# Spare products in TensorE's gaps, grouped transfers of the totals and a re-planned order, in a gated linear attention with a low-rank mixer behind it

## The chip, the cores and the metric

The kernel runs on one core of one Trainium2 chip. The metric is device time in microseconds (us), the median of several executions; lower is better. The engines are TensorE (PE, with its weight loads shown as PEld), VectorE (DVE), ScalarE (ACT), GpSimd (POOL) and SyncE (SP), which here only issues transfers. All data is float32. L12 is line 12 of the kernel whose profile is read.

## The reference

Two stages follow each other. The first is an attention with a complex gate, for 4 batches, 8 heads, 768 steps, 48 channels:

```python
mag = np.sqrt(a_re * a_re + a_im * a_im)
scale = np.minimum(mag, 0.999) / (mag + 1e-06)
a_re_n, a_im_n = (a_re * scale, a_im * scale)
for t in range(S):
    new_re = ar * S_re - ai * S_im            # ar, ai: step t of a_re_n, a_im_n
    new_im = ar * S_im + ai * S_re
    S_re, S_im = (new_re + k[t] outer v[t], new_im)
    y[:, :, t] = q[t] @ S_re
```

The second takes y as x (4 x 768 x 384) and mixes it, over time by a product of rank 32, and over channels by two layers (384 to 1536 and back):

```python
h = xt @ U @ V                                # xt: x with time last
u = x + h.transpose(0, 2, 1)
ch = np.maximum(u @ w_ch1, 0.0) @ w_ch2
return u + ch
```

## The kernel before

**Chunks.** Time is cut into chunks of 128 steps, 6 per batch, 24 in all. They are numbered 0 to 23. The gates are computed for groups of chunks: two groups of one chunk, then groups of two (`GROUPS`).

**Stages of the attention, per group or chunk.**
- `gates(g)`: magnitudes and logarithms of the gates on ACT and DVE (tiles x, y, l in GL, n); `within`: product `es ps` (L513) and two exponentials es; `totals`: products `tot` (L529), an exponential into E, and four transfers T<-E per chunk on SP's queue (L536), which put E's four blocks of rows into T's layout; `turns`: the angles z, then product `ph` (L569, and L572 for the carry of the first batch's chunks), then ACT and DVE make F, the fraction of a turn. From the second batch on a small transfer of POOL's queue adds the last row of F to the next chunk's z (z<-F, L563). `waves`: sine and cosine cs.
- `prep(i)`: DVE multiplies q and k by es and cs (qkc); PE transposes (`tr`, L618); ACT copies into QK.
- `chain(i)`: DVE multiplies QK by T at growing distances (L297); between them PE makes the products of the diagonal (`inner`, L652), `corners` (L699) and `corner` (L714), which go to AT, in part by way of DG and four transfers AT<-DG (L689); `ks ps`, `yT` (L748, L752), `dk` (L762) and G carry the state; `yr` (L777) turns the result back to xo.

**The mixing.** `mixer(m)` treats two chunks. Its first one of a batch needs all six chunks' xo (`rank`, L802). Then `mixed` (L814) and `uTp` (L821) make uT; 36 products `up` (L833, six at a time) with a Relu on ACT into h, and 12 `down` (L844) per chunk; DVE adds; POOL's queue writes the output (L850). The weights w1 and w2 are given as float64: `single` loads each panel as words (raw), six DVE operations turn them into float32, and a transfer of POOL's queue adds the remainder.

**What sets the order.** No loop above issues instructions. Each operation is given to `Plan` with its engine, a cost, what it reads and writes, the tiles it takes and a rank, and `Plan.order` simulates the five engines: whenever an engine is free, it picks among the operations that are ready and whose buffers are free the one with the lowest urgency (of the table `URGENCY`, by kind and number), and among those within 4 of it (`stay`) one of the same `way`, which is 1 for products that use a part of the array. The order found is issued as it is: every engine works through its own list, and an instruction waits there for its inputs with all that is behind it. The costs are formulas (`c_act`, `c_dve`, `c_dma`); `SP` adds 2.0 until a transfer lands, and `PE` multiplies by 1.3 for the first six chunks. "small" (the mixing's small steps) has urgency n - 1000, "mixing" (up, down) n + 1000, so that up and down are what PE does when it has nothing else. A buffer is taken in the plan by the first operation that reads or writes it.

Of the kernel before, what the change touches and what calls it, by code (L numbers as in the profile page):

```python
# [25 lines left out]
    "w1": {0: 22.6, 1: 16.9, 2: 21.7, 3: 31.9, 4: 26.8, 5: 7.2, 6: 29.2},  # L26
    "w2": {0: 30.9, 2: 32.1, 4: 29.2, 6: 36.2, 8: 31.1, 10: 46},
    "gates": {0: -14.2, 1: 4.3, 2: -3.3, 4: 4.1, 6: 26.6, 8: 13.4, 10: 16.1, 12: 17.5, 14: 17.8, 16: 24.3, 18: 23.5,
        20: 24.3, 22: 26.5},
    "angles": {0: -6, 1: 1.4, 2: 1.1, 4: -0.7, 6: 9.1, 8: 15.2, 10: 15.7, 12: 17.1, 14: 17.4, 16: 30.3, 18: 23.2,  # L30
        20: 12.9, 22: 26.4},
    "totals": {0: -98.9, 1: -100.2, 2: -95.1, 3: -104.8, 4: -93, 5: -92, 6: -97.8, 7: -99.3, 8: -88.1, 9: -93.3,
        10: -90.1, 11: -91, 12: -87.6, 13: -93.2, 14: -86.5, 15: -82.1, 16: -87.3, 17: -82.3, 18: -76.1, 19: -78,
        20: -75.7, 21: -76.5, 22: -77.2, 23: -78.7},
    "prep": {0: -3.4, 1: -6.1, 2: -1.7, 3: -0.5, 4: 1, 5: 2.1, 6: 8.3, 7: 9.2, 8: 10.3, 9: 11, 10: 13.2, 11: 14.9,
        12: 16.1, 13: 15.9, 14: 16.6, 15: 18.2, 16: 18, 17: 19.5, 18: 11, 19: 21, 20: 21.6, 21: 21.9, 22: 16.5,
        23: 33.7},
    "levels": {0: 0.6, 1: -3.8, 2: 0.6, 3: -1.7, 4: -1.9, 5: -1.5, 6: 8.4, 7: 8.6, 8: 6.8, 9: 14.9, 10: 12.7, 11: 13,
        12: 13.2, 13: 17.8, 14: 12.3, 15: 13.3, 16: 20.7, 17: 20.5, 18: 19.3, 19: 16.6, 20: 21.5, 21: 20.9, 22: 20.7,
        23: 28.2},  # L40
    "rest": {0: 7.1, 1: 3.2, 2: 4.6, 3: 6.2, 4: 5.8, 5: 6.4, 6: 7.8, 7: 13.7, 8: 16.8, 9: 17.2, 10: 14.8, 11: 18.2,
        12: 21, 13: 22.1, 14: 22.6, 15: 26, 16: 25.3, 17: 26.7, 18: 23, 19: 26.1, 20: 26.1, 21: 29.8, 22: 27.9,
        23: 30.6},
# [3 lines left out]
class Plan:  # L47
# [5 lines left out]
    def __init__(self, lag, change, stay, urgency):  # L53
        self.lag, self.change, self.stay, self.urgency = lag, change, stay, urgency
        self.ops, self.log, self.tag, self.bufs = [], {}, {}, {}
# [5 lines left out]
    def add(self, engine, cost, rank, f, reads=(), writes=(), late=0.0, way=0):  # L61
# [3 lines left out]
        need, uses = set(), set()  # L65
# [11 lines left out]
    def order(self):  # L77
# [15 lines left out]
        events, out, now = [], [], 0.0  # L93
# [16 lines left out]
        while True:  # L110
            for e in free:
# [17 lines left out]
                if pick:  # L129
# [15 lines left out]
            while events and events[0][0] <= now:  # L145
                _, n, landed = heapq.heappop(events)
                if landed:
# [8 lines left out]
        assert len(out) == len(ops), "the plan is stuck"  # L156
# [4 lines left out]
def kernel(  # L161
# [65 lines left out]
    plan = Plan(0.06, 0.12, 4.0, urgency)  # L227
# [44 lines left out]
    def ACT(*a, **kw):  # L272
        plan.add("ACT", *a, **kw)

    def DVE(*a, **kw):
        plan.add("DVE", *a, **kw)
# [4 lines left out]
    def SP(*a, **kw):  # L281
        plan.add("SP", *a, late=2.0, **kw)
# [7 lines left out]
    def switch(rank, name):  # L290
        table(1.28, rank, lambda: nc.scalar.preload_act_table_set(name))  # L291
# [668 lines left out]
```

## Time and profile before

| | |
|---|---|
| median of 3 runs | 792.26 us (790.36 to 792.93) |
| the profiled execution's own time | 786.05 us |
| its span, first to last instruction | 784.3 us |
| mean granted clock of TensorE | 0.961 of full |
| PE busy | 711.5 us (91%) |
| DVE, ACT, POOL busy | 428.9, 398.8, 45.3 us |
| first `up` on PE | 164.37 us after the span's start |
| T<-E, transfers | 96, of 48 KB each |

The profile is of one execution. Its page gives busy time by engine, the span in 40 slices with the granted clock of TensorE in tenths, the chain of work that ended last followed back from the last instruction, and groups of instructions with the idle time before them and what ended it. Its trace can be asked for the timeline of an engine, the waits of an engine by what ended them, and the busy time of all engines in given stretches. An f32 product stands in the records as two passes, a transpose as one. In the first 30 us the clock's record reads 1.00.

### The profile page before, as it was taken

The numbers are of one execution on the slowest core, as the hardware profiler recorded it, in microseconds if no ns is written. First come the engines' busy times: TensorE is split into PE (matmuls) and PEld (weight loads), VectorE is DVE, ScalarE is ACT, GpSimd is POOL, SyncE is SP. The second block draws the span as 40 slices with busy tenths as digits, with TensorE's granted clock in tenths as the row PEclk, the third lists the DMA queues.
The fourth block names the chain that finished last, engine by engine and source line by source line (L and its number), as shares of the span: only waits on it lengthen the run. The fifth ranks groups of instructions, "written<-read, shape, count | busy, mean of one in ns | idle before, by whom it ended". The sixth has DMA issues, their size and how long they took to land.

```text
span 784.3 us, 21460 instructions
## 1 busy us (share of the span) xinstructions
PE 711.5 (91%) x9522; PEld 535.4 (68%) x9522; DVE 428.9 (55%) x585; ACT 398.8 (51%) x686; POOL 45.3 (6%) x83
## 2 busy tenths in 40 slices
PE   2657877788989999999999999999999999999996
PEld 0435656566678868867876787676886867677683
DVE  5797988867859686585867883552623010010100
ACT  6586867665767686949596765241321202011010
POOL 4000000111000000000000000000000000000000
PEclk9857989899989999999999999999999999999999
DMA  8867536747432333333314312110100000000000
GB/s 192 188 129 160 100 90 138 152 120 161 89 79 43 73 70 70 76 58 70 80 38 106 69 37 55 42 26 11 41 1 18 11 11 11 20 1 21 10 11 20
DMA packets 165500, 52.89 MB, mean 67 GB/s; under 512 B 154784, under 2 KB 160416, under 8 KB 165408
## 3 DMA queue, kind: packets, MB, share of 16 engines
q1 hardware_dynamic: 161520, 41.87, 24.6%
q0 software_dynamic: 3888, 9.66, 5.1%
q8 instruction: 75, 1.23, 0.7%
q14 instruction: 17, 0.14, 0.1%
HBM read 33.59 MB, written 4.72 MB: 49 GB/s over the span
## 4 chain that ended last, share of the span: by engine, by line
PE 78%; DVE 7%; ACT 5%; DMA 4%; issue 4%; SPq 1%; POOL 0%; POOLq 0%; DVEq 0%; ACTq 0%
PE up L833 23%; PE down L844 22%; PE tr L618 5%; PE inner L652 5%; PE dk L762 3%; DVE QK L297 3%; PE ph L569 2%; PE yT L748 2%; PE es ps L513 2%; PE yT L752 2%; PE corner L714 2%; PE corners L699 2%; PE mixed L814 2%; PE ks ps L734 1%; PE tot L529 1%
## 5 line engine op out<-in xcount | busy, mean ns | idle before, releaser
L844 PE MATMUL down<-w,h 128*128 128x384 f32 x576 | 199.2, 489 | 0.0
L833 PE MATMUL up<-uT,w 128*128 128x256 f32 x864 | 196.9, 384 | 0.0
L297 DVE TENSOR_TENSOR QK<-QK,T 96x1024 f32<-96x1024 f32 (+1 forms) x144 | 169.6, 1186 | 20.4 <-PE corner L714 10.2
L833 PEld LDWEIGHTS up<-uT,w 128*128 128x128 f32 x864 | 162.8, 191 | 24.9 <-issue 1.0
L844 PEld LDWEIGHTS down<-w,h 128*128 128x128 f32 x576 | 104.9, 190 | 60.4 <-issue 0.2
L294 ACT ACTIVATE h<-up 128x512 f32<-128x512 f32 x72 | 42.9, 596 | 160.5 <-PE up L833 160.3
L652 PEld LDWEIGHTS inner<-QK 96*32 96x32 f32 x4608 | 48.3, 113 | 36.2 <-issue 26.2
L652 PE MATMUL inner<-QK 96*32 96x16 f32 (+1 forms) x4608 | 55.6, 192 | 13.6 <-DVE QK L297 8.8
L618 PE MATMUL tr<-ident,qkc 128*96 128x128 f32 x384 | 57.4, 291 | 10.9 <-DVE qkc L297 10.1
L300 DVE TENSOR_TENSOR xo<-mixed,xo 128x384 f32<-128x384 f32 x24 | 13.2, 555 | 95.5 <-PE mixed L814 94.7
L297 DVE TENSOR_TENSOR qkc<-qk,cs 128x768 f32<-128x768 f32 x48 | 45.8, 953 | 32.7 <-PE tr L618 23.2
L618 PEld LDWEIGHTS tr<-ident,qkc 128*96 128x96 f32 x384 | 44.4, 134 | 26.3 <-DVE qkc L297 10.0
L300 DVE TENSOR_TENSOR xo<-down,xo 128x384 f32<-128x384 f32 x24 | 13.3, 556 | 89.4 <-PE down L844 89.4
L621 ACT COPY QK<-tr 96x512 f32<-96x512 f32 x96 | 52.4, 581 | 18.4 <-PE tr L618 18.1
L658 DVE COPY_PREDICATED DG<-mask,inner 128x128 f32<-128x128 int32 (+1 forms) x72 | 24.6, 343 | 32.1 <-PE inner L652 29.9
L748 PE MATMUL yT<-AT,VP 128*64 128x128 f32 x384 | 37.7, 280 | 4.8 <-DMA AT<-DG 2.3
L779 ACT COPY xo<-yr 128x384 f32<-128x384 f32 x24 | 11.5, 478 | 56.1 <-DMA out_dram<-xo 50.7
L513 PE MATMUL es ps<-GL,mid 128*128 128x384 f32 x48 | 23.5, 599 | 15.2 <-DVE GL L500 14.0
L850 POOL DMA_DIRECT2D out_dram<-xo x24 | 13.5, 562 | 394.0 <-DVE xo L300 386.8
L762 PEld LDWEIGHTS dk<-VP,ks 128*96 128x96 f32 x320 | 31.7, 173 | 3.3 <-issue 2.0
L291 ACT ACT_TABLE_LOAD x26 | 33.4, 1283 | 1.2 <-PEq L944 0.7
L762 PE MATMUL dk<-VP,ks 128*96 128x48 f32 x320 | 33.1, 256 | 0.0
(93 smaller groups left out, 842.9 us busy)
## 6 DMA issues: line engine op xcount, KB each, us to landing
ar<-in_a_re_dram SPq DMA_DIRECT2D x24, 192.0 KB, 3.4
ai<-in_a_im_dram SPq DMA_DIRECT2D x24, 192.0 KB, 3.4
raw<-in_moe_w_ch_dram SPq DMA_DIRECT2D x6, 768.0 KB, 5.3
qk<-in_q_dram SPq DMA_DIRECT2D x24, 192.0 KB, 2.9
qk<-in_k_dram SPq DMA_DIRECT2D x24, 192.0 KB, 3.5
VP<-in_v_dram SPq DMA_DIRECT2D x24, 192.0 KB, 3.2
w<-cx POOLq DMA_DIRECT2D x12, 384.0 KB, 5.8
T<-E SPq DMA_DIRECT2D x96, 48.0 KB, 2.0
```

Of the source, the lines that this page charges most:

```text
L291: table(1.28, rank, lambda: nc.scalar.preload_act_table_set(name))
L294: return nc.scalar.activation(out=o, in_=i, func=f, **kw)
L297: nc.vector.tensor_tensor(out=o, in0=a, in1=b, op=OP.mult)
L300: nc.vector.tensor_tensor(out=o, in0=a, in1=b, op=OP.add)
L513: PE(0.65, R1, lambda: nc.tensor.matmul(out=get(*ps), lhsT=mid, rhs=of(l, i), start=True, stop=True), [l, ("mid", 0)], [ps, ("sums", g, i)])
L618: nc.tensor.transpose(out=get(*ps)[0:D2, j], in_=get(*qkc)[:, hh * HH + j].rearrange("p u d -> p (u d)"), identity=ident)
L621: ACT(c_act(HH * CH) - 0.05, R1, lambda u=u, hh=hh, ps=ps: nc.scalar.copy(out=get(*QK)[:, u, hh * HH:(hh + 1) * HH], in_=get(*ps)[0:D2]), ...
L652: nc.tensor.matmul(out=get(*ps)[js, h], lhsT=k_of(h)[:, js], rhs=part(q_of(h)[:, js], "p"), start=True, stop=True, tile_position=(0, j * BLK))
L748: nc.tensor.matmul(out=a[u * DP:(u + 1) * DP, p], lhsT=vv[:, h], rhs=get(*ATi)[:, h], start=True, stop=(c == 0), tile_position=(0, u * DP))
L762: nc.tensor.matmul(out=get(*dk)[0:D2, h], lhsT=get(*ks)[:, h], rhs=get(*VPi)[:, h, 0:D], start=True, stop=True)
L833: nc.tensor.matmul(out=get(*ps)[:, e], lhsT=w1[:, f, (ff + e) * 128:(ff + e + 1) * 128], rhs=get(*uT)[:, f], start=(f == 0), stop=(f == KD ...
L844: nc.tensor.matmul(out=get(*ps), lhsT=get(*h)[:, ff, cc * CH:(cc + 1) * CH], rhs=w2[:, ff], start=(ff == 0), stop=(ff == KF - 1))
```

## The change

1. **Spare products.** From 3 us of the plan's time on and until the first up, whenever PE has nothing to do in the plan, a product of the identity with itself is put there (cost 0.3). It writes a tile of PSUM that nobody reads. The order has 188 of them.
2. **Totals by group.** E and T hold a group; T has 3 buffers of a group in place of 6 of a chunk, E one of a group in place of two of a chunk. The four transfers move both chunks at once: 52 transfers in place of 96. They have a fixed urgency, as have the transfers AT<-DG (`"place"`), which stood at the rank of "rest".
3. **The plan's rules.** PE costs are no longer multiplied by 1.3 and have 0.17 until they land; ACT and DVE give 0.09 of their cost to landing; SP issues cost at least 0.65 and land 1.4 or 2.0 later; a product that follows on PE may start when the one before it has been issued. `takes`: a product takes the buffer that its result will go to. The operations on one ACT table may change places between two table loads.
4. **Loads.** U is loaded by one transfer for six, each panel of w2 by one for two.
5. **New numbers** for all kinds in `URGENCY`.

The order that comes out, at three places. First TensorE at the start of the program (es ps, tot and ph belong to the gates of chunk 0, tr to its q and k). Before:

```order
L513 MATMUL es ps<-GL,mid 128x384
L529 MATMUL tot<-total,GL 64x64 x8
L569 MATMUL ph<-z,prefix 128x384
L618 MATMUL tr<-ident,qkc 96x128 x16
L513 MATMUL es ps<-GL,mid 128x384
L652 MATMUL inner<-QK 32x32 x32
```

and in the change:

```order
L924 MATMUL spare<-ident 128x128 x20
L522 MATMUL es ps<-GL,mid 128x384
L548 MATMUL tot<-total,GL 64x64 x8
L924 MATMUL spare<-ident 128x128 x13
L580 MATMUL ph<-z,prefix 128x384
L924 MATMUL spare<-ident 128x128 x19
L630 MATMUL tr<-ident,qkc 96x128 x8
L924 MATMUL spare<-ident 128x128 x5
```

The real products stand in the same order, with runs of spare ones between them.

Second, TensorE around the first up, with the last products of the first batch's attention ahead of it (yr) and the mixing's rank, mixed and uTp. Before:

```order
L777 MATMUL yr<-ident,yTs 128x128 x4
L569 MATMUL ph<-z,prefix 128x384
L802 MATMUL rank<-xo,UV 32x384 x6
L814 MATMUL mixed<-r,V 128x384 x2
L821 MATMUL uTp<-ident,xo 128x128 x6
L569 MATMUL ph<-z,prefix 128x384
L833 MATMUL up<-uT,w_64 128x256 x12
```

and in the change:

```order
L815 MATMUL rank<-xo,UV 32x384 x6
L548 MATMUL tot<-total,GL 64x64 x8
L924 MATMUL spare<-ident 128x128
L827 MATMUL mixed<-r,V 128x384 x2
L924 MATMUL spare<-ident 128x128
L834 MATMUL uTp<-ident,xo 128x128 x3
L924 MATMUL spare<-ident 128x128
L834 MATMUL uTp<-ident,xo 128x128 x3
L924 MATMUL spare<-ident 128x128 x3
L846 MATMUL up<-uT,w_64 128x256 x6
L580 MATMUL ph<-z,prefix 128x384
L846 MATMUL up<-uT,w_64 128x256 x12
```

The two ph products (of chunks 6 and 7, whose z may come from POOL's queue) stood ahead of the first up and now stand behind its first six and its next twelve. Ahead of the first up PE has otherwise the same products in both.

Third, SP's queue where the first group of two chunks has its totals. Before:

```order
L396 DMA ar<-in_a_re_dram 128x8x48 x2
L396 DMA ai<-in_a_im_dram 128x8x48
L536 DMA T<-E 48x256 x8
L396 DMA ai<-in_a_im_dram 128x8x48
L423 DMA raw<-in_moe_w_ch_dram 128x1536
L423 DMA raw<-in_moe_U_dram 128x64 x6
```

and in the change:

```order
L535 DMA T<-E 48x2x256 x2
L701 DMA AT_99<-DG_100 32x8x32 x4
L535 DMA T<-E 48x2x256 x2
L409 DMA qk<-in_k_dram 128x8x48
L411 DMA VP_89<-in_v_dram 128x8x48
L402 DMA ar<-in_a_re_dram 128x8x48 x2
L402 DMA ai<-in_a_im_dram 128x8x48 x2
L430 DMA raw<-in_moe_w_ch_dram 128x1536
L430 DMA raw<-in_moe_U_dram 128x6x64
```

Eight transfers of totals became four, all of the group's gate loads (ar, ai) now stand behind them, and U is one transfer.

The diff, cut:

```diff
 URGENCY = {
-    "w1": {0: 22.6, 1: 16.9, 2: 21.7, 3: 31.9, 4: 26.8, 5: 7.2, 6: 29.2},
+    "w1": {0: 100.39, 1: -28.13, 2: 97.08, 3: 85.64, 4: 58.8, 5: 15.35, 6: 28.72},
...
-    "totals": {0: -98.9, 1: -100.2, 2: -95.1, 3: -104.8, 4: -93, 5: -92, 6: -97.8, 7: -99.3, 8: -88.1, 9: -93.3,
...
-    def add(self, engine, cost, rank, f, reads=(), writes=(), late=0.0, way=0):
+    def add(self, engine, cost, rank, f, reads=(), writes=(), late=0.0, way=0, takes=()):
...
-        need, uses = set(), set()
+        need, uses = set(), {a[:2] for a in takes}
...
+                    mixing = mixing or ops[n][3][0] == "mixing"
+                elif e == "PE" and now >= self.idle[0] and free[e] <= now and events and not mixing:
+                    out.append(-1)
+                    free[e] = now + self.idle[1]
+                    ways[e] = 0
+                    heapq.heappush(events, (free[e], -1, 0))
...
-                    if (ops[m][0] != ops[n][0] or ops[n][2] > 0) == bool(landed):
+                    if (ops[m][0] != "PE" or ops[n][0] != "PE") == bool(landed):
...
-        if kind == "totals":
+        if kind in ("totals", "place"):
             return n - 100
...
-    plan = Plan(0.06, 0.12, 4.0, urgency)
+    plan = Plan(0.04, 0.12, 4.0, (3.0, 0.3), urgency)
...
-    def PE(cost, rank, *a, **kw):
-
-        plan.add("PE", cost * (1.3 if rank[0] not in ("small", "mixing") and rank[1] < NCH else 1.0), rank, *a, **kw)
...
+    def PE(*a, **kw):
+        plan.add("PE", *a, late=0.17, **kw)
+
+    def ACT(cost, *a, **kw):
+        plan.add("ACT", cost - 0.09, *a, late=0.09, **kw)
+
+    def DVE(cost, *a, **kw):
+        plan.add("DVE", cost - 0.09, *a, late=0.09, **kw)
...
-    def SP(*a, **kw):
-        plan.add("SP", *a, late=2.0, **kw)
+    def SP(cost, *a, **kw):
+        plan.add("SP", max(cost, 0.65), *a, late=2.0 if cost > 0.65 else 1.4, **kw)
...
-        ACT(cost, rank, f, reads=reads, writes=list(writes) + [TABLE])
+        ACT(cost, rank, f, reads=list(reads) + [TABLE], writes=writes)
...
+        def totals():
+            e, tt = ("E", g), ("T", g)
+            buffer(e, "E", 1, [128, GC, HH, NTOT])
+            buffer(tt, "T", 3, [D2, GC, H * NTOT])
+            for i in range(lo, hi):
+                of_blocks(i)
+            for u in range(2):
+                for w in range(2):
+                    SP(0.65, ("totals", lo), lambda u=u, w=w: nc.sync.dma_start(
+                        out=get(*tt)[u * D:(u + 1) * D, 0:hi - lo, w * HH * NTOT:(w + 1) * HH * NTOT],
+                        in_=get(*e)[w * 64:w * 64 + D, 0:hi - lo].rearrange("p c h b -> p c (h b)")), [e], [tt + ((u, w),)])
...
-            SP(0.15, RR, lambda js=js: nc.sync.dma_start(out=get(*ATi)[js, :, js], in_=get(*DGi)[js]), [DGi],
+            SP(0.65, ("place", i), lambda js=js: nc.sync.dma_start(out=get(*ATi)[js, :, js], in_=get(*DGi)[js]), [DGi],
...
+    spare = []
+
+    def idle():
+
+        if not spare:
+            spare.append(pools["psM"].tile([128, 128], FP, tag="psM", name="spare", padded_shape=[128, 512]))
+        nc.tensor.matmul(out=spare[0], lhsT=ident, rhs=ident, start=True, stop=True)
     for n in plan.order():
-        plan.ops[n][4]()
+        (plan.ops[n][4] if n >= 0 else idle)()
```

More of the change, by code (lines that the diff above doesn't have):

```diff
@@ L92, in order @@
         have = set()
-        events, out, now = [], [], 0.0
+        events, out, now, mixing = [], [], 0.0, False
         def fits(n):
@@ L155, in order @@
                             heapq.heappush(ready[ops[m][0]], (rank[m], m))
-        assert len(out) == len(ops), "the plan is stuck"
+        assert len(out) == len(ops) + out.count(-1), "the plan is stuck"
         return out
@@ L671, in f @@
                 mul(qk, qk, tp)
[L672 removed]
+            DVE(c_dve((u1 - u0) * H * CH // 2), rank, f, [("T", group_of(i))], [QK])
         def grow(rank, hf, u0=0, u1=2):
```

112 lines of the change are left out of this document (51 added, 61 removed).

## The prediction

> **What bounds the kernel now.** I read the page first: the busy shares, the slices, and the shares of the chain that ended last.
>
> ```profile
> span 784.3 us, 21460 instructions
> PE 711.5 (91%) x9522; PEld 535.4 (68%) x9522; DVE 428.9 (55%) x585; ACT 398.8 (51%) x686; POOL 45.3 (6%) x83
> PE   2657877788989999999999999999999999999996
> PEclk9857989899989999999999999999999999999999
> PE 78%; DVE 7%; ACT 5%; DMA 4%; issue 4%; SPq 1%; POOL 0%; POOLq 0%; DVEq 0%; ACTq 0%
> ```
>
> TensorE is the bound, but not everywhere: its slices are full from about the twelfth on, and before that they stand at 2 to 9 tenths, with a granted clock that falls to half. So I asked for the busy time in stretches cut at the first product of the mixing (164.4 us), and for the end. Columns: stretch and length, busy time and instructions of PE, its weight loads, DVE, ACT, POOL, then the clock, the DMA share and GB/s.
>
> ```profile
> 0.00:40.00 40.00, 17.49 (x282) 11.01 (x282) 26.25 (x49) 25.06 (x45) 10.17 (x33) 0.91 0.81 190
> 40.00:100.00 60.00, 40.01 (x840) 31.60 (x840) 52.51 (x72) 48.93 (x80) 3.41 (x4) 0.77 0.62 130
> 100.00:165.00 65.00, 48.98 (x928) 35.83 (x929) 52.49 (x72) 41.92 (x72) 3.40 (x4) 0.88 0.55 127
> 164.00:784.00 620.00, 606.04 (x7475) 457.53 (x7474) 297.63 (x394) 283.25 (x490) 28.32 (x42) 0.99 0.21 47
> 761.85 15.64 PE L844 MATMUL down<-w,h 128*128 128x384 f32 x48
> 777.53 0.56 DVE L300 TENSOR_TENSOR xo<-down,xo 128x384 f32<-128x384 f32 x1 [7.18 <-PE down L844]
> ```
>
> Once the mixing has begun, PE is busy for 606.0 us of the 613 until its last product ends at about 777.4. That work is the same in both kernels. So the span is the time of the first mixing product, plus about 613 us of PE work, plus a fixed tail of 7 us (777.5 to 784.3). What the change is worth is how much earlier that first product comes (**first up**, below), and what it does to the 7 us of idle PE behind it.
>
> Ahead of first up no engine is full: PE 106.5 of 165 us, DVE 131.3, ACT 115.9. The chain of waits in that stretch alternates between them:
>
> ```profile
> by line: DVE QK L297 11.8%; issue 8.3%; PE tr L618 5.7%; PE ph L569 5.6%; DMA z<-F 4.5%; DVE qkc L297 4.5%; PE es ps L513 3.7%; PE inner L652 3.5%; ACT y L294 3.4%; ACT L291 3.1%; PE ph L572 3.1%; ACT x L294 2.4%; ACT GL L294 2.1%; DMA VP<-
> ```
>
> **Part 1: the clock ahead of first up.** The timeline shows the same groups at half and at full clock:
>
> ```profile
> 48.25 1.91 PE L618 MATMUL tr<-ident,qkc 128*96 128x128 f32 x8 [0.50 <-DVE qkc L297]
> 54.36 2.92 PE L513 MATMUL es ps<-GL,mid 128*128 128x384 f32 x4 [4.20 <-DVE GL L500]
> 57.22 2.16 PE L529 MATMUL tot<-total,GL 128*64 128x64 f32 x32
> 170.40 1.45 PE L513 MATMUL es ps<-GL,mid 128*128 128x384 f32 x4
> 174.38 1.15 PE L529 MATMUL tot<-total,GL 128*64 128x64 f32 x32
> 435.67 1.08 PE L618 MATMUL tr<-ident,qkc 128*96 128x128 f32 x8
> 438.47 0.60 PE L618 MATMUL tr<-ident,qkc 128*96 128x128 f32 x4
> ```
>
> tr goes from 1.91 to 1.08 us, es ps from 2.92 to 1.45, tot from 2.16 to 1.15. On the chain before 165 us, tr, es ps and the two ph lines hold 5.7 + 3.7 + 5.6 + 3.1 = 18.1%, or 29.9 us; nearly all of their pieces ran cold, and at the warm ratio (0.5 to 0.57) about 13 us of that goes, and with tot (1 us) and the cold pieces of dk, corners and ks (an estimate of 1 us) **15 us**. That is the upper end: all of it counts only if nothing else takes over. What can take over is DVE, which works 52.5 of the 60 us from 40 to 100. The lower end is 0, if DVE is the true bound there and PE's pieces stand on the chain by turns only. I take the middle, **-7.5 us**: DVE is idle for about 30 us before the first product of the mixing, some 7 of them at the start, before data is there.
>
> Do the spare products hold the clock up? Three stretches of 5 us say how little it takes to lose it:
>
> ```profile
> 125.00:130.00 5.00, 3.46 (x159) 3.08 (x159) 3.00 (x5) 3.46 (x5) 0.00 (x0) 1.00 0.53 134
> 130.00:135.00 5.00, 3.89 (x135) 3.46 (x131) 4.22 (x5) 2.03 (x5) 0.00 (x0) 1.00 0.70 131
> 135.00:140.00 5.00, 5.00 (x95) 3.23 (x94) 3.36 (x6) 2.59 (x7) 0.00 (x0) 0.66 0.67 125
> ```
>
> Busy for 7.35 of 10 us, PE is throttled in the next 5, though no single idle stretch there was long (the chain's waits inside it are of 1.5 us). The planned spare products stand in just such gaps, so I expect most, not all, of the clock.
>
> [...]
>
> **What the spare products cost.** There are 188, all ahead of first up. Eight tr against four cost 1.08 - 0.60 = 0.48 us more, so one pass of 128 columns takes 0.12 us. An f32 product is two passes (the page has 864 records for the 432 products of up), so a spare takes 0.24 us warm and, at tr's ratio, 0.43 us cold: 45 us in all warm, 81 cold. The room: PE's 106.5 us carry a cold surcharge of about 24 us (half-clock shares of 46% and 24% from the clocks 0.77 and 0.88; the first 40 us taken as cold), so the real work is 82.7 us, and a first up at about 149 leaves 66 us of gaps. 45 fits, with 21 to spare. Each spare stands where the plan sees PE idle for at least an instant, so a real product that comes early waits for at most the run ahead of it. I cost them at **0**; the price without that cover is the third rival. They stop at first up, so they take nothing from the 613 us.
>
> **Part 2: SP's queue.** Four transfers per group in place of eight. Before:
>
> ```profile
> 58.80 6.83 SPq L536 DMA_DIRECT2D T<-E  x8
> 65.67 0.58 SPq L396 DMA_DIRECT2D ai<-in_a_im_dram  x1
> 65.00:70.00 5.00, 2.69 (x76) 1.79 (x74) 1.88 (x2) 1.59 (x3) 0.85 (x1) 1.00 0.72 145
> ```
>
> Eight issues hold SP for 6.8 us (0.85 each), the load of ai stands behind them, and from 65 to 70 us PE, DVE and ACT are all mostly idle. Four fewer are 3.4 us at most on that place. The four now start only when both chunks' totals stand, and move twice the bytes, so part of it goes back. **-2 us**, between -3.4 and 0. U as one transfer for six and w2 as one for two save issues too; SP had idle time there, 0.
>
> **Part 3: what stands in front of first up.** The place itself, before:
>
> ```profile
> 153.53 2.61 PE L802 MATMUL rank<-xo,UV 128*32 128x384 f32 x12
> 156.75 1.56 PE L814 MATMUL mixed<-r,V 128*128 128x384 f32 x4 [0.61 <-ACT r L805]
> 158.31 1.19 PE L821 MATMUL uTp<-ident,xo 128*128 128x128 f32 x6
> 158.90 1.20 DVE L823 COPY uT<-uTp 128x384 f32<-128x384 f32 x2
> 162.96 1.62 PE L569 MATMUL ph<-z,prefix 128*128 128x384 f32 x2 [3.45 <-DMA z<-F]
> 164.37 5.98 PE L833 MATMUL up<-uT,w 128*128 128x256 f32 x23
> 149.66 0.95 DVE L548 SCALAR_TENSOR_TENSOR z<-x,n 128x768 f32<-128x768 f32 x1
> 154.25 0.55 DVE L575 SCALAR_TENSOR_TENSOR F<-F,ph 128x384 f32<-128x384 f32 x1 [0.59 <-ACT F L294]
> 154.98 0.96 DVE L300 TENSOR_TENSOR x<-x,y 128x768 f32<-128x768 f32 x1 [0.18 <-ACT y L294]
> 155.98 0.56 DVE L490 TENSOR_SCALAR x<-x 128x768 f32<-128x768 f32 x1
> ```
>
> The mixing's input uT is complete at 160.1, but PE stands in a ph that waits for its z (a transfer that lands late), so up starts at 164.37 and not at 160.2: **-4.2 us**, since in the change both late ph products stand behind the first six ups. If z is late there as well, PE waits in the mixing instead and the gain is 0; it is nearer to the full gain, because z's transfer then has the time of six ups more. The two ph products are work moved behind first up: 1.62 us cold, by es ps's ratio 0.8 us warm, so **+1.6 us** for both.
>
> DVE has the same work ahead of the first add of the mixing but for one z, one F, one sum and one clamp of x, which now come later: 0.95 + 0.55 + 0.96 + 0.56 = 3.0 us. As DVE is full for only part of this stretch I count half, **-1.5 us** (0 to -3).
>
> **Part 4: behind first up.** PE's waits there, the largest:
>
> ```profile
> PE yT L748 <- DMA AT<-DG: 2.3, 1, 2.3
> PE tot L529 <- issue: 1.6, 1, 1.6
> ```
>
> All of them make about 7 us. A new order may lose these or bring others of the same size; I take **0**, with -7 and +7 as bounds. The plan's durations, the buffers it takes early, E as one buffer of a group (where ACT must now wait for four transfers to land before the next group's exponentials) and the freer table order act only through the order; behind first up DVE has 298 and ACT 283 us of work in 620, which hides it. Were that cover gone, PE would wait for tr or inner inputs, as it does before 165.
>
> **Sum.** -7.5 - 2 - 4.2 - 1.5 + 1.6 = -13.6 us: first up at about 149, span 770.7 us. The profiled execution took 786.05 us in all (1.75 outside its span), so it would be 772.5; the runs shown have a median of 792.26, 0.8% above it, and I take the same 13.6 us from that: **778.7 us**.
>
> **Rivals.**
> - *DVE is the bound* and the clock is not. The clock's 7.5 and SP's 2 us go; 4.2 + 1.5 - 1.6 = 4.1 us stay: **788 us**. For it: 52.5 of 60 us. Against it: DVE's 30 idle us, and that PE's lines hold more of the chain than any.
> - *The clock is full from the start* and the whole 15 us come off: 792.26 - 13.6 - 7.5 = **771 us**. Against it: the throttling at 135 us, without a long gap, and DVE.
> - *Slower: the spares stay cold and PE falls behind its plan.* PE's demand ahead of first up is (82.7 + 45) us at full clock and, cold, 1.77 times that. With a half-clock share f it is 127.7 x (1 + 0.77 f): it overtakes 164.4 us at f = 0.37, which is a mean granted clock of about 0.81 up to first up. At 0.75 (f = 0.5) it is 177, 12.5 us later than before, with the 1.6 of ph **806 us**. For it: the clock was 0.77 from 40 to 100 with PE busy for two thirds. [...]
>
> **How the numbers follow.** Forecast 0.47 (between 772 and 785 by the ends of its terms), DVE the bound 0.24, full clock 0.15, cold spares 0.14. The range 764 to 790 holds the forecast, most of the full clock's case and of the DVE case: about 8 in 10. What a measurement of this kernel can tell from no change is 0.3%, 2.4 us: 789.9 to 794.6 is the same. Faster: 0.46 + 0.15 + 0.17 = 0.78. Same: 0.07 of the DVE case, and 0.02 of the others, 0.09. Slower: 0.13.
>
> **What would show it.** Right: a clock above 0.95 up to first up, tr x8 near 1.1 us at 50 us, first up between 145 and 153, and some 613 us from there to PE's last product. The clock at one and first up near 160 is DVE's case; a clock below 0.81 with spares right in front of late products is the slow one; new PE waits over 7 us behind first up would break the term I set to nothing.

## The result and the profile after

| | before | after |
|---|---|---|
| median | 791.31 us (788.90 to 792.93, 4 runs) | 767.96 us (766.59 to 773.01, 4 runs) |
| ratio | | 0.9721, 95% interval 0.9676 to 0.9765 |
| profiled execution, its span | 786.05, 784.3 us | 773.01, 771.2 us |
| second profile, its span | 789.77, 788.0 us | 765.88, 764.1 us |
| first up, in the two profiles | 164.37, 164.22 us | 150.71, 148.61 us |

The change makes the kernel 23 us faster. The forecast was 778.7 us, with 764 to 790 as its range. Before was run again beside the experiments, 7 to 17 executions at a time, and its medians were then 787.7 to 788.6 us; against these the gain is some 20 us.

The page of the changed kernel, with the span, the busy time by engine, the slices of TensorE and of its granted clock, and the group of the spare products:

```profile
span 771.2 us, 22118 instructions
PE 740.9 (96%) x9898; PEld 572.5 (74%) x9898; DVE 424.2 (55%) x585; ACT 393.4 (51%) x686; POOL 44.9 (6%) x83
PE   8989998997999999999999999999999999999996
PEclk9999898999999999999999999999999999999999
L924 PE MATMUL spare<-ident 128*128 128x128 f32 x376 | 57.6, 302 | 1.7 <-POOL ident masks.py:199 1.4
```

The first eleven slices of PE stood at 2 to 9 tenths and read 7 to 9 now, and the clock's slices there read 8 and 9, where they read 5 to 9. Take the 57.6 us of spares from the 740.9 and the same real products take 683.3 us, where they took 711.5. I put these 28.2 us down to the clock, since the same groups run in about half the time (es ps and tr, below). The span fell by 13.1 us only, so PE's gaps (idle and spares together) grew by 15.1, from 72.8 to 87.9 us. More than half of what the warmer TensorE saves is spent waiting for the others.

The stretches of the changed kernel (columns as in the prediction: PE, its weight loads, DVE, ACT, POOL, clock, DMA share, GB/s) and pieces of its timeline:

```profile
40.00:100.00 60.00, 54.22 (x1081) 45.07 (x1080) 52.19 (x72) 44.63 (x76) 2.57 (x3) 0.94 0.69 147
0.00:150.70 150.70, 135.67 (x2420) 116.00 (x2420) 124.49 (x186) 107.17 (x189) 16.27 (x40) 0.95 0.66 144
150.00:771.00 621.00, 605.90 (x7485) 457.07 (x7483) 300.29 (x402) 286.86 (x499) 28.61 (x43) 0.99 0.23 51
1.45 7.13 PE L924 MATMUL spare<-ident 128*128 128x128 f32 x40 [1.45 <-POOL ident masks.py:199]
9.79 0.88 PE L522 MATMUL es ps<-GL,mid 128*128 128x384 f32 x2 [1.21 <-DVE GL L509]
11.22 3.17 PE L924 MATMUL spare<-ident 128*128 128x128 f32 x26
36.40 1.04 PE L630 MATMUL tr<-ident,qkc 128*96 128x128 f32 x8
150.71 2.86 PE L846 MATMUL up<-uT,w 128*128 128x256 f32 x12
160.80 0.91 PE L580 MATMUL ph<-z,prefix 128*128 128x384 f32 x2 [1.41 <-DMA z<-F]
```

The clock from 40 to 100 us went from 0.77 to 0.94, tr from 1.91 to 1.04 us, the first es ps from 1.62 to 0.88 us, and first up waits for no z. One of the two ph waits now inside the mixing, 1.41 us. Behind first up this pair shows no gain: PE's last product ends 6.8 us ahead of the span's end in all four profiles, which gives 613.1 us before (784.3 - 164.4 - 6.8) and 613.7 after (771.2 - 150.7 - 6.8).

That pair alone would say that Part 4 was right. But the profiled execution of before was one of its quicker ones, that of after the slowest of four. The second profile of each is nearer to the medians. Their stretches, before and then after:

```profile
164.00:788.00 624.00, 609.54 (x7475) 459.96 (x7473) 297.76 (x394) 283.70 (x490) 27.92 (x42) 0.98 0.21 47
```

```profile
0.00:148.60 148.60, 136.17 (x2420) 116.80 (x2420) 124.59 (x186) 107.14 (x189) 16.26 (x40) 0.94 0.67 147
148.00:764.00 616.00, 603.81 (x7484) 456.24 (x7482) 299.98 (x401) 286.59 (x499) 28.93 (x43) 1.00 0.23 51
```

From first up to PE's last product it is 617.0 us before (PE's last product at 781.2) and 608.7 after (757.3). So 788.0 became 764.1 us by 15.6 us ahead of first up and **8.3 us behind it**. Both figures are from one profile each. Four more runs have the change's order behind first up, with 610.2, 608.1, 607.5 and 609.8 us there (experiments 1, 4, 9 and 10). The mean of all six is 609.7 us, that of the two of before 615.1, and the order of before has 611.3 in experiment 2. So the gain behind first up is nearer to 5 us than to 8.3, and it differs from execution to execution.

One place holds most of the 8.3 us of this pair. Before, in its second profile, first on PE, then on SP's queue, then the stretches of 3.41 us around it:

```profile
216.50 0.82 PE L734 MATMUL ks ps<-ident,QK 96*128 96x96 f32 x8
219.88 1.74 PE L748 MATMUL yT<-AT,VP 128*64 128x128 f32 x16 [2.55 <-DMA AT<-DG]
209.46 6.18 SPq L536 DMA_DIRECT2D T<-E  x8
215.74 4.75 SPq L689 DMA_DIRECT2D AT<-DG  x7
216.75:220.16 3.41, 0.86 (x13) 0.70 (x13) 1.83 (x3) 0.86 (x2) 0.57 (x1) 1.00 0.45 109
...
226.99:230.40 3.41, 3.41 (x9) 2.69 (x9) 1.49 (x2) 3.06 (x4) 0.82 (x1) 0.50 0.15 28
```

yT waits 2.55 us for the transfers AT<-DG, which SP issues only behind eight T<-E (6.18 us). PE was busy for 0.86 of 3.41 us there, and it runs at half clock for the next 10.24 us (the three stretches up to 230.40), which costs about 5.1 us more: 7.7 us for a wait that the list of waits shows with 2.6. The profile in the prediction has the same place (2.3 us, the row yT <- AT<-DG), with 6.8 us at half clock from 220.7 us on. A further 2.3 us of the pair lie right behind first up, where half clock follows the wait for z: the first 24 passes of up take 7.69 us before, and 24 passes in the change 5.34. After, in its second profile, on SP's queue and PE:

```profile
200.63 3.62 SPq L535 DMA_DIRECT2D T<-E  x4
208.76 3.08 SPq L701 DMA_DIRECT2D AT<-DG  x4
214.47 1.09 PE L760 MATMUL yT<-AT,VP 128*64 128x128 f32 x16
```

T<-E is four issues, four AT<-DG stand ahead of it (at 195.16 us) and four behind, yT waits for nothing and the clock stays. The halving of T<-E is not what did this: with eight again in the change's order yT does not wait either (experiment 5). What remains is the new order, of SP's queue and of PE; which of the two is not shown.

### The profile page after: what moved, and what is told of

It reads as the page before. It is cut to its first block, busy times and chain, and to the rows that moved or that the text cites. A ratio compares the mean times of both kernels' runs of the same rounds, so it can differ in the third digit from the quotient of the medians.

```text
span 771.2 us, 22118 instructions
## 1 busy us (share of the span) xinstructions
PE 740.9 (96%) x9898; PEld 572.5 (74%) x9898; DVE 424.2 (55%) x585; ACT 393.4 (51%) x686; POOL 44.9 (6%) x83
## 3 DMA queue, kind: packets, MB, share of 16 engines
q8 instruction: 78, 1.28, 0.7%
## 4 chain that ended last, share of the span: by engine, by line
PE 71%; ACT 9%; issue 8%; DVE 6%; DMA 4%; SPq 1%; POOL 1%; POOLq 0%; DVEq 0%; ACTq 0%
PE down L857 21%; PE up L846 20%; PE inner L664 5%; PE tr L630 4%; PE dk L775 3%; PE yT L760 2%; PE es ps L522 2%; PE yT L764 2%; PE spare L924 2%; DVE QK L303 2%; DMA z<-F 2%; ACT x L300 2%; PE ph L580 2%; PE mixed L827 1%; ACT L297 1%
## 5 line engine op out<-in xcount | busy, mean ns | idle before, releaser
L846 PEld LDWEIGHTS up<-uT,w 128*128 128x128 f32 x864 | 161.0, 190 | 24.7 <-issue 1.0
L924 PE MATMUL spare<-ident 128*128 128x128 f32 x376 | 57.6, 302 | 1.7 <-POOL ident masks.py:199 1.4
L630 PE MATMUL tr<-ident,qkc 128*96 128x128 f32 x384 | 53.2, 279 | 2.7 <-DVE uT L836 1.0
L924 PEld LDWEIGHTS spare<-ident 128*128 128x128 f32 x376 | 50.9, 210 | 4.5 <-POOL ident masks.py:199 1.4
L630 PEld LDWEIGHTS tr<-ident,qkc 128*96 128x96 f32 x384 | 41.6, 128 | 10.6 <-issue 2.6
L764 PE MATMUL yT<-QK,G 96*48 96x128 f32 x320 | 31.7, 272 | 0.0
```

The source lines that it names most:

```text
L630: nc.tensor.transpose(out=get(*ps)[0:D2, j], in_=get(*qkc)[:, hh * HH + j].rearrange("p u d -> p (u d)"), identity=ident)
L764: nc.tensor.matmul(out=a[u * DP:u * DP + D, p], lhsT=get("G", i - 1)[:, h], rhs=q_of(h), start=False, stop=True, tile_position=(0, u * DP))
L846: nc.tensor.matmul(out=get(*ps)[:, e], lhsT=w1[:, f, (ff + e) * 128:(ff + e + 1) * 128], rhs=get(*uT)[:, f], start=(f == 0), stop=(f == KD ...
L924: nc.tensor.matmul(out=spare[0], lhsT=ident, rhs=ident, start=True, stop=True)
```

## The experiments

Ratios are to the kernel before on the same chip, with 95% intervals. "Behind" is the time from first up to PE's last product.

**1. The spares alone, taken from the change.** The order of all real instructions is kept.

```diff
     for n in plan.order():
-        (plan.ops[n][4] if n >= 0 else idle)()
+        if n >= 0:
+            plan.ops[n][4]()
```

> The changed kernel without its 188 spare products; every other instruction stands in the same order. Theory (the clock): most of the gain hangs on the clock that the spares hold up. Mean granted clock from 0 to 145 us falls from 0.95 to about 0.85, the first up comes 10 to 16 us later than 150.7, and the time is 778 to 785 us. Rival (the order): the new order and its rules brought the gain, the spares only fill idle time; the first up stays within 4 us of 150.7 and the time is 765 to 772 us.

776.70 us (774.68 to 779.15), ratio 0.9841 (0.9793 to 0.9889). The spares are worth 0.9841 - 0.9721 = 0.012, 9.5 us by the ratios and 8.7 by the medians; with the two intervals, 4 to 15 us. First up at 155.88 us, 610.2 behind. Neither expectation holds as it stands: the theory asked for 778 to 785 us and a first up at least 10 us later, the rival for 765 to 772 us. The profile without spares:

```profile
40.00:100.00 60.00, 43.03 (x877) 30.62 (x876) 52.61 (x71) 45.22 (x75) 2.58 (x3) 0.81 0.70 147
9.79 1.62 PE L522 MATMUL es ps<-GL,mid 128*128 128x384 f32 x2 [9.79 <-DVE GL L509]
```

The clock is 0.81 in place of 0.94. The first es ps starts at 9.79 us with twenty spares ahead of it and without: these delay nothing. By the ratios more than half of the gain, 0.016 of 0.028, comes without spares.

**2. Spares alone, added to the order before.** 147 fit into its plan's gaps.

```diff
+                    if e == "PE" and not mixing:
+                        out += [-1] * max(0, int((now - last) / 0.3))
...
-        plan.ops[n][4]()
+        (plan.ops[n][4] if n >= 0 else idle)()
```

> The kernel before, its order unchanged on every engine, with 147 spare products put into the gaps that its own plan shows on PE from 3 us to the first up. Theory (the clock): 8 to 15 us faster than before, 776 to 783 us, tr x8 near 1.05 us from 45 us on, and the wait for z in front of the first up still there. Rival (the order): no more than 4 us from before, 787 to 792 us.

779.76 us (778.76 to 780.88), ratio 0.9879 (0.9837 to 0.9921): 9.6 us, as expected and close to experiment 1. First up at 159.57, 4.7 us earlier than before, 611.3 behind. The wait for z in front of first up is still there (4.0 us), and so is the one for AT<-DG:

```profile
PE yT L753 <- DMA AT<-DG: 2.3, 1, 2.3
```

but no half clock followed it in this execution, so what the spares gave behind first up cannot be told from where a wait happens to fall.

**3. The change with the urgencies of before.** Rules, grouped totals and 212 spares stay.

```diff
-    "w1": {0: 100.39, 1: -28.13, ...
+    "w1": {0: 22.6, 1: 16.9, ...
...
```

> The changed kernel with the urgencies of before; the plan's new rules, the four transfers per group and the spares (212 of them in this order) stay. Theory (the clock): the clock is held as in the changed kernel, and the numbers bring a few us: 769 to 776 us. Rival (the order): the numbers bring most of the gain, 780 to 790 us.

775.34 us (771.65 to 778.86), ratio 0.9819 (0.9755 to 0.9882): the new numbers are worth about 0.01, 8 us (with the two intervals, 2 to 14). Its stretches, and first up:

```profile
100.00:145.00 45.00, 40.32 (x886) 34.98 (x884) 40.54 (x56) 33.51 (x61) 2.31 (x3) 1.00 0.66 143
145.00:161.00 16.00, 13.35 (x74) 8.53 (x76) 11.43 (x20) 10.51 (x17) 1.80 (x2) 0.79 0.64 138
161.26 2.86 PE L849 MATMUL up<-uT,w 128*128 128x256 f32 x12
```

The clock is full from 100 to 145 us and first up comes at 161.26 all the same, 11 us later than in the change, while the kernel is 8 us slower. Behind it are 606.2 us, the least of all: its order has two es ps, two ph and eight tot more ahead of first up, and PE waits for 1.9 us behind. In part, first up and the stretch behind it trade with each other.

**4. Each spare as two transposes** of the same size.

```diff
-        nc.tensor.matmul(out=spare[0], lhsT=ident, rhs=ident, start=True, stop=True)
+        for _ in range(2):
+            nc.tensor.transpose(out=spare[0], in_=ident, identity=ident)
```

> The changed kernel with each spare product replaced by two transposes of the identity, one pass of 128 columns each as a spare has two; they too are read by nobody. If a transpose holds up the clock as a product does: the clock to the first up stays at 0.95 and the time within 4 us of the changed kernel's 768. If it does not: as without spares by the theory, 778 to 785 us, with tr x8 near 1.9 us in many places before 100 us.

766.59 us (762.29 to 773.18), ratio 0.9719 (0.9653 to 0.9785), the same as the change. First up at 145.63. The opening's forty transposes, and the stretch:

```profile
1.46 6.56 PE L925 MATMUL spare<-ident 128*128 128x128 f32 x40 [1.46 <-POOL ident masks.py:199]
40.00:100.00 60.00, 55.14 (x1120) 45.43 (x1120) 55.07 (x75) 47.65 (x81) 2.58 (x3) 0.97 0.68 146
```

Transposes hold the clock at 0.97, and they bring it up as well: in the opening, where PE has run nothing else yet, they start 0.213 us apart up to 5.5 us and 0.109 us apart from there on. So in this kernel a transpose holds up the clock as a product does: 0.97 from 40 to 100 us, where the change has 0.94 and experiment 1, without spares, 0.81.

**5. Eight transfers per group again**, the change's order kept: each of the four T<-E of a group of two is issued as two.

```diff
-                    SP(0.65, ("totals", lo), lambda u=u, w=w: nc.sync.dma_start(
-                        out=get(*tt)[u * D:(u + 1) * D, 0:hi - lo, ...
+                    SP(0.65, ("totals", lo), lambda u=u, w=w: [nc.sync.dma_start(
+                        out=get(*tt)[u * D:(u + 1) * D, c, ...
+                        in_=get(*e)[w * 64:w * 64 + D, c]...) for c in range(hi - lo)], ...
```

> The changed kernel, its order held, with the totals of a group of two chunks in eight transfers (one per chunk and block) in place of four, at the same place of SP's queue. The prediction's term for the four transfers (2 us, between 0 and 3.4): 768 to 771 us. Rival, that SP's queue is off the path once the order is new: within 1 us of the changed kernel, and the load of ai still lands before ACT asks for it.

776.14 us (774.91 to 777.43), ratio 0.9850 (0.9789 to 0.9911): 8 us slower than the change by the medians, 0.013 by the ratios, and slower than either expectation. SP's queue with eight, and in the change with four:

```profile
51.13 5.00 SPq L535 DMA_DIRECT2D T<-E  x4
58.91 3.25 SPq L535 DMA_DIRECT2D T<-E  x4
```

```profile
52.40 1.75 SPq L535 DMA_DIRECT2D T<-E  x2
58.41 1.25 SPq L535 DMA_DIRECT2D T<-E  x2
```

Eight issues hold SP for 8.25 us, four for 3.0 at the same place. First up is at 152.31, 1.6 to 3.7 us later than in the two profiles of the change, as the prediction sized it. The other part stands behind: 616.0 us with 11 us of waits, where the change has 613.7 and 608.7 with 8.1 and 5.1. The largest new wait:

```profile
PE ph L581 <- DVE uT L837: 3.0, 1, 3.0
```

The wait of yT for AT<-DG does not come back: eight T<-E hold SP for 6.10 us from 204.30 on, four AT<-DG follow at 213.08, and yT starts at 218.79 us without a wait.

The order in this run was planned for four, so the 8 us are the price of eight under this order, not of grouping under any.

**6. The wait for z.** The plan is told that z<-F lands 7.0 us late, not 1.6.

```diff
-                     [("F", i - 1)], [zi], late=1.6)
+                     [("F", i - 1)], [zi], late=7.0)
```

> The changed kernel with one cost of the plan changed: the small transfer z<-F is planned to land after 7.0 us in place of 1.6, so that the products ph move back in PE's order (the first ones by six ups more). If PE's waits for z behind the first up (4.7 us in the profile of the changed kernel) are on the path, 3 to 5 us faster: 763 to 766 us. Rival: the order shifts elsewhere and takes it back, 766 to 772 us.

765.94 us (764.14 to 768.12), ratio 0.9713 (0.9641 to 0.9785). The waits for z behind first up are gone (4.7 and 2.8 us in the two profiles of the change), and the time, at the edge of both expectations, cannot be told from the change's. The new order brought other waits, 4.2 us in all.

**7 and 8. Both kernels once more**, unchanged, for a second profile. The windows of 3.4 us are those of the clock's record: in the first profile of before its stretches of half clock up to the mixing last 3.41, 6.83, 10.24 or 17.07 us, which is one, two, three or five times 3.41.

> The kernel before once more, for a second profile: the one that the prediction read took 786.05 us, 5 us under the median. Theory: what differs from execution to execution is the clock ahead of the first up, by the place at which the clock's windows of 3.4 us fall; a slower execution has more half-clock windows or longer stops of PE, and its PE work from the first up to the end is again 613 to 620 us. Rival: the difference lies behind the first up.

> The changed kernel once more, for a second profile: the first took 773.01 us, 5 us over the median. Theory: the stops of PE inside inner's bursts and the half-clock windows that follow them fall elsewhere or are shorter; first up at 145 to 149 us and 765 to 769 us in all. Rival: the first up stays at 150 to 151 us and the difference lies behind it.

789.77 and 765.88 us: these are the second profiles of the section on the result. Before has its first up at the same time in both, and the difference of 3.7 us lies behind it (613.1 and 617.0 us), as the rival had it. Of the 7.1 us between the two profiles of the change 2.1 lie ahead of first up and 5.0 behind it; both theory and rival have a part.

**9. Every second spare left out.**

```diff
-        (plan.ops[n][4] if n >= 0 else idle)()
+        if n >= 0:
+            plan.ops[n][4]()
+        else:
+            count += 1
+            if count % 2:
+                idle()
```

Ahead of first up the clock fell in the first profile of before behind stretches of 3.41 us with 0.25 to 1.16 us of PE's work and behind one with 2.30, and in that of the change behind 1.53 and 1.54 us.

> The changed kernel with every second spare product left out (94 of 188), all else in the same order. Theory (the clock falls behind a window of 3.4 us in which PE was busy for less than about half): the half keeps some windows above the mark and loses others; more falls before the first up than the two or three of the changed kernel, fewer than the seven without spares; 769 to 774 us. Rival (any filling of long gaps is enough): clock and time as in the changed kernel, 765 to 769 us.

768.31 us (767.02 to 769.78), ratio 0.9763 (0.9711 to 0.9815). The interval holds the change's ratio, so 94 spares do about as much as 188. The clock is lower, though:

```profile
40.00:100.00 60.00, 48.41 (x1005) 37.74 (x1004) 52.64 (x71) 44.50 (x75) 2.58 (x3) 0.91 0.70 149
```

0.91 from 40 to 100 us, with first up at 151.53. Ahead of first up the clock falls six times, against two and three times in the two profiles of the change and seven times without spares (experiment 1), as the theory had it; the time lies in the rival's range. The last hundredths of the clock there bring little. That DVE then sets the pace, with 52.64 us of work in 60, would explain it and is not shown. What was expected of either theory lies within 5 us here, and the run does not separate them well.

**10 and 11. PE's stops.** In the change PE stops inside bursts of inner while the profile names nothing that it waits for ("issue"):

```profile
114.64 0.53 PE L664 MATMUL inner<-QK 96*32 96x32 f32 x36
117.23 0.45 PE L664 MATMUL inner<-QK 96*32 96x32 f32 x28 [2.06 <-issue]
123.00 0.94 PE L664 MATMUL inner<-QK 96*32 96x16 f32 x52 [2.31 <-issue]
```

Counted in PE's own order (products, weight loads and semaphore instructions, from 0), the product behind each such stop in inner has a number that leaves 193 or 194 by 256, in this profile and in the first of before. The page has 78 transfers of instructions, of 16.4 KB each, for PE's 19970 instructions: one for every 256. In experiment 10 the first three spares are dropped, 12 instructions of PE; in experiment 11, 21 narrow products of 32 columns are put between the opening's spares, 84 instructions more.

```diff
+        seen += n < 0
...
+        elif seen > 3:
+            idle()
```

```diff
+        idle()
+        if narrow:
+            narrow -= 1
+            nc.tensor.matmul(out=spare[0][0:32, 0:32], lhsT=ident[:, 0:32], rhs=ident[:, 0:32], ...)
```

> The changed kernel without the first 3 of its 20 opening spares, 12 PE instructions fewer, which moves every later instruction 12 places ahead in the blocks of 256 in which the instructions are fetched. Theory (PE stops where a block of 256 ends inside a burst of short products): the stops at 77, 113 and 120 us move or shrink, at most two stops over 0.5 us are left before the first up, and the time is 1 to 4 us under the changed kernel's, 763 to 767 us. Rival (the stops hang on the transfers at that time, not on the place in the block): they stay at 77, 113 and 120 us and the time stays at 766 to 769 us.

> The changed kernel with 21 narrow products (32 by 32, unread) between its opening spares: 84 PE instructions more and about 2.5 us of PE at a place where PE waited for 1.2 to 2.2 us. By the blocks of 256, twice as many ends as in the changed kernel fall into bursts of inner. Theory: more stops before the first up, each again 192 places into a block, and 2 to 6 us over the changed kernel, 769 to 774 us. Rival (the stops hang on the transfers at that time): stops as before, 766 to 769 us.

Experiment 10: 768.01 us (765.81 to 770.44, 6 runs), ratio 0.9758 (0.9720 to 0.9797). The stop moved by just the 12 instructions, six passes (three products) further into the burst:

```profile
112.78 0.58 PE L664 MATMUL inner<-QK 96*32 96x32 f32 x42
115.06 0.39 PE L664 MATMUL inner<-QK 96*32 96x32 f32 x22 [1.71 <-issue]
```

So it belongs to the number of the instruction, not to the data. The stop at 77 us is gone, and the two others shrink, from 2.06 and 2.31 us to 1.71 and 1.17. The time did not gain from the shift, against the expectation.

Experiment 11: 783.04 us (778.34 to 791.02, 12 runs), ratio 0.9946 (0.9914 to 0.9978), 15 us slower than experiment 10 beside it. Ahead of first up PE's stops take 3.4 us in all, less than the change's 6.2, where more was expected. What made the run slow is the opening:

```profile
1.45 0.79 PE L924 MATMUL spare<-ident 128*128 128x128 f32 x2 [1.45 <-POOL ident masks.py:199]
2.17 0.32 PE L933 MATMUL spare<-ident 128*32 128x32 f32 x2
2.42 0.80 PE L924 MATMUL spare<-ident 128*128 128x128 f32 x2
...
20.91 1.65 PE L522 MATMUL es ps<-GL,mid 128*128 128x384 f32 x2
ACT es L300 <- PE es ps L522: 12.3, 1, 12.3
```

A spare with a narrow one behind it took 0.97 us. In the change's opening the passes of a spare start 0.213 us apart up to 6.5 us and 0.112 us apart from there on, which is 0.43 us a spare at half clock and 0.22 at the full one. Here the opening stayed at half clock: es ps takes 1.65 us, as without spares (1.62 us, experiment 1), where the change has 0.88. The full clock comes at 28.5 us, behind the first stretch of 3.41 us that holds full-width spares alone. The first es ps came at 20.91 in place of 9.79 us, ACT waited 12.3 us for it, and first up came at 158.66. This is the prediction's slow rival, in the opening alone: the spares stay cold, and PE falls behind its plan. The clock's mean over the span, 0.99, does not show it, since the record has no entry ahead of 28.5 us and the view reads 1.00 there.

**12. The moved ph alone**, in the kernel before: the first two groups of up stand ahead of the ph of chunk 7.

```diff
-    for n in plan.order():
+    seq = plan.order()
+    ups = [n for n in seq if plan.ops[n][3][0] == "mixing"][:2]
+    at = max(k for k, n in enumerate(seq[:seq.index(ups[0])]) if plan.ops[n][3][0] == "angles" and plan.ops[n][0] == "PE")
...
+    seq = [n for n in seq[:at] if n not in ups] + ups + [n for n in seq[at:] if n not in ups]
+    for n in seq:
```

> The kernel before with one thing moved: the first two groups of six up stand ahead of the ph of chunk 7 in TensorE's list (before: rank, mixed, uTp, ph, up x12, es ps; here: rank, mixed, uTp, up x12, ph, es ps). No spare products, nothing else changed; it computes the same. It is Part 3 alone, for one of the two ph. Theory: first up comes right behind uT, at 160 to 161 us in place of 164.2 to 164.4, the z of that ph lands under the ups, and the ph itself costs 0.8 us behind them: 3.4 us less; the window of half clock that follows PE's wait for z in both profiles of before (from 162 us on) goes too, up to 1.7 us more. Ratio to before 0.993 to 0.996, 3 to 5 us. Rival: the wait is moved, not taken away. The es ps and ph behind need what ACT and DVE make, and the mixing of the first two chunks runs out of it later by as much: the first up is earlier, the stretch behind it longer by the same 3 to 4 us, and the ratio lies within 0.3% of 1.

789.62 us (784.23 to 794.62, 12 runs), before 788.46 (17 runs), ratio 1.0003 (0.9974 to 1.0031). Here, and then in the second profile of before:

```profile
161.08 5.45 PE L833 MATMUL up<-uT,w 128*128 128x256 f32 x24 [0.65 <-DVE uT L823]
170.49 2.90 PE L513 MATMUL es ps<-GL,mid 128*128 128x384 f32 x4 [3.31 <-DVE GL L500]
```

```profile
162.81 1.62 PE L569 MATMUL ph<-z,prefix 128*128 128x384 f32 x2 [3.24 <-DMA z<-F]
164.22 7.69 PE L833 MATMUL up<-uT,w 128*128 128x256 f32 x24
171.75 1.45 PE L513 MATMUL es ps<-GL,mid 128*128 128x384 f32 x4
```

First up is 3.1 us earlier and the wait for z is gone. But the es ps behind is now the one that waits, 3.31 us for GL from DVE, and runs at half clock (2.90 us against 1.45). The stretch behind first up is 620.7 us, 617.0 in the second profile of before. The rival had it: the wait is moved, not taken away.

## Why the prediction was right, and where it was wrong

The side was right, and the range held the time. The median fell by 23 us, or by some 20 against the later runs of before, where 13.6 were forecast.

- **First up.** 149 was forecast; it is 150.71 and 148.61, from 164.37 and 164.22. The sum ahead of first up holds. Of the signs named for it tr near 1.1 us came; the clock, 0.94 to 0.95 where "above 0.95" was asked for, just missed; and the 613 us behind first up are 613.7 and 608.7.
- **Part 4, behind first up, set to 0, is the term that failed.** Some 5 us are gained there, 8.3 in the pair of second profiles. The prediction had the row (yT waits 2.3 us for AT<-DG) and took it as an item of some 7 us of waits that any new order would replace. What it left out is that this wait drags the clock down for 7 to 10 us behind it, in a stretch where PE has no slack. The fall is in the profile of before, 6.8 us of it. The sign named for this term, new waits of over 7 us, could not show it: the waits behind first up are 7.3 and 7.2 us before, 8.1 and 5.1 after, and most of the difference is in the clock.
- **Part 2, -2 us, was sized at one place.** Ahead of first up the four issues less give 1.6 to 3.7 us, within the bounds of 0 to 3.4 or nearly, though the row that it calls mostly idle has PE busy for 2.69 of its 5 us. Over the whole kernel eight issues in place of four cost 8 us (experiment 5), and the range of the term did not reach there, because only the stretch to first up was looked at. That run does not have the wait of Part 4, so these 8 us stand in other waits; how many of them an order planned for eight would save is open.
- **Part 1, -7.5 us.** The spares measured 9.5 us in the change and 9.6 on the order before, within the bounds of 0 and 15. That they cost nothing is right where it can be read: the first es ps starts when it did (experiment 1). Of the 0.24 us a spare, forecast from tr, the run at 11.22 us has 3.17 for 13.
- **Part 3, -4.2 us.** The mechanism (first up behind uT, the ph behind it) is seen, but alone it is worth 0 to the end, between 2.1 us less and 2.4 us more (experiment 12). It was counted as if the 613 us behind first up were fixed.
- **The model itself.** "First up plus 613 us" is what joins these: experiments 3 and 12 move first up and the stretch behind it against each other. Read at first up alone, the parts come near their terms: the spares 5.2 to 7.3 us of 7.5 (experiment 1), the transfers 1.6 to 3.7 of 2, the moved ph 3.1 of 4.2. But the new urgencies had no term, and with those of before first up comes 11 to 13 us later at a nearly full clock (experiment 3). These effects overlap, so that the sum ahead of first up came out is in part luck.
- **The rivals.** The time is nearest to the full clock's 771, but its mechanism is not seen: the clock is 0.94 to 0.95 up to first up and some 15 of the 28 us that PE's products save come back as gaps. DVE as the bound: its sign, a full clock with first up near 160, came in experiment 3, with a kernel 13 us faster than before, so that sign was a bad one. That DVE limits what more clock can bring in the change is argued (experiment 9). The cold spares did not come in the change; experiment 11 has them.

What stays open: how the gain splits between rules, urgencies and grouping, since each order is a new plan and the parts (9.5, 8 and 8 us) add up to more than the whole; and how much of the gain behind first up comes in every execution, since it is read from single profiles.

## What to carry to other kernels

A wait on a full engine is to be priced with what follows it: 2.55 us of idle time cost 7.7 here, as the clock stood at half for the next 10.24 us, while a like wait of 2.3 us cost 2.3 in experiment 2. A model of the form "start of the bound stretch plus its work" holds only as long as that stretch has no waits and no work that can be pushed into it; test it by moving one product, as in experiment 12, ahead of pricing a dozen. Spare products were cheap here where the plan saw a gap (the first es ps starts at 9.79 us with and without them, experiment 1), and half of them did as much (768.31 us); full-width ones, products or transposes, were the cheap ones, and with narrow ones among them the opening stayed at half clock (es ps at 20.91 us took 1.65 us, experiment 11).

## What the hardware showed that was not expected

**The clock falls behind a half-busy stretch.** The recorded clock has two values, 1.00 and 0.50, and changes on a grid of 3.41 us. Its record begins late: at 29.6 us in the first profile of before, and at 6.5 us in the change, where the passes of the spares go from 0.213 to 0.112 us; ahead of that the views read 1.00. On that grid, in the changed kernel:

```profile
119.15:122.56 3.41, 1.53 (x46) 1.29 (x34) 1.54 (x3) 0.67 (x2) 0.00 (x0) 1.00 0.57 196
122.56:125.98 3.42, 2.98 (x88) 2.69 (x88) 1.42 (x2) 0.00 (x0) 0.00 (x0) 0.50 0.31 79
```

PE was busy for 1.53 of 3.41 us, and the next stretch ran at half. Up to 250 us, over all 14 profiles, the recorded clock fell behind every stretch with up to 1.77 us of busy time; with 1.79 to 1.87 it did either; from 1.89 on it stayed, with two exceptions (2.30 and 2.31, in bursts of the narrow inner, one in each profile of before). It came back only behind stretches with 2.74 us or more, and not behind every one: in the second profile of before the two full stretches from 220.16 us did not bring it back. Nor is busy time in the records the whole of it: in the opening of experiment 11 PE reads as busy for all of every stretch from 4.58 to 25.06 us, and es ps at 20.91 us still took 1.65 us, as at half clock. The grid explains why a wait of 2.3 us costs 2.3 (experiment 2) and one of 2.55 us 7.7: the first is shared by two stretches, which keep 2.16 and 2.35 us of work, and the clock stays at 1.00; the second lies in one, which keeps 0.86.

**PE stops at fixed instruction numbers.** In the first profiles of before and of the change ten stops of 0.47 to 2.31 us, with nothing awaited, lie inside bursts of inner. The products behind them stand at 193 or 194 by 256 in PE's order, and in experiment 10 the stop moved with that number. The page of the change has 78 transfers of instructions with 1.28 MB, 16.4 KB each:

```profile
q8 instruction: 78, 1.28, 0.7%
```

The change has 19970 instructions of PE, 78.0 times 256; before has 19241, 75.2 times 256, and 75 transfers. In the two traces all ten stops end 2.3 to 2.6 us after the start of one of these transfers, whatever their own length. That PE waits there for its next instructions is my reading of these times and is not shown, since no run takes the transfers away. The stop of 2.31 us that ends at 123.00 lies for the most part in the stretch ahead of 122.56 us, behind which the clock fell.
